# Narrower loads, half-block inversion in two groups and 512-token units in a recurrent-attention and feed-forward kernel

## The chip, the cores and the metric

The kernel runs on one core of one Trainium2 chip. The metric is the device time in microseconds (us) of one execution; lower is better. The engines are named as the profile names them: PE (TensorE matmul), PEld (TensorE weight load), DVE (VectorE), ACT (ScalarE), POOL (GpSimd) and SP (SyncE, which here only issues DMAs).

## The reference, cut to what matters

Two parts follow each other. The first is a recurrence over 768 tokens for each of 4 x 8 heads with a 40 x 40 state; the second multiplies its 3072 x 320 output through two up-projections, an elementwise product and a down-projection of width 1536 (weights in 64-bit floats).

```python
for t in range(S):                                    # S = 768, D = 40
    y[:, :, t] = np.einsum('bhd,bhde->bhe', rt, state)
    Sa = np.einsum('bhde,bhe->bhd', state, at)
    state_decay = state * wt[:, :, None, :] - np.einsum('bhd,bhe->bhde', Sa, bt)
    state = state_decay + np.einsum('bhd,bhe->bhde', vt, kt)
...
a = x @ w_a; b = x @ w_b; out = (a * b) @ w_out       # x: 3072 x 320, d_ff = 1536
```

## The kernel before, in words

**Attention in chunks.** The 768 tokens are cut into `NS` = 12 chunks of `C` = 64. Within a chunk the recurrence becomes matrix products and the inverse of a unit triangular 64 x 64 matrix for each head. Each chunk is handled in two parts c = 0, 1 (`NP`) of 16 heads, so there are 24 pairs (n, c), numbered q. In SBUF two heads share the 128 partitions: each half of 64 rows holds the 40 channels of a head and 24 rows of padding.

- `prep(n, c)` loads `W` (decays), `BK` (b and k) and `A` (a), runs two scans over the decays on DVE, scales the inputs, forms the score matrices on PE (`scores`), copies them to `AB` and `TK`, transposes `BK` on PE (`nat`, with the helper `transp`), and writes five results to a scratch area `un_d` in DRAM. `size` squares and sums two of them on ACT for a check of range.
- `lanes(g)` inverts the 32 x 32 diagonal blocks of two chunks at once (`GROUPS`: six groups of two): a transpose on DVE to `Nt`, then 31 steps of one multiplication and one subtraction on DVE over `Yt` (rows `Wt` are named Yt in the profile), then two transposes, `TC` and `T3` (named T in the profile). The code holds a second form, taken for the groups in `HALVED` (empty before): 15 steps over two 16 x 16 blocks at once, after which `join(n)` builds the 32 x 32 inverse on PE in three stages (`xt`, `t3`, `tc_`), with ACT copies between them.
- `merge(n)` builds the 64 x 64 inverse `T` from the 32 x 32 ones with two stages of small matmuls (`l2a`, `l2b`).
- `main(n, c)` loads `un_d` back (`UN`), v by token (`SV`, through `load_v`) and r, v by channel (`RV`), copies the state `ST` into the rest of `SV` on ACT (`s0`), and computes in turn `r_`, `u_`, the new state (`s_`, DVE), `g_`, `y_` and the outputs `X`, which go through DRAM (`x_d`) so that `pack(n)` can lay out the feed-forward input `xk` (its high and low parts).

**Feed-forward in units.** `unit` takes one tile f of 128 of the 1536 columns (`NF` = 12 tiles) and one chunk of 256 tokens: 16 matmuls into `ab` (2 x 8, 256 columns each), an ACT copy and a DVE product `g`, a rounded copy `gh` (ACT) and its remainder `gl` (POOL), and 6 matmuls of 320 columns into `po` (`second`). There are 144 units. The first `F1` = 5 tiles are done for each chunk while the attention runs; their sums go to DRAM (`po_d`) and come back as `acc` later. The other 7 tiles, in groups of `FG` = 2, run over all 12 chunks after the attention, and `xk` of the first 11 chunks is stored to `xk_d` and reloaded for this. The weights are decoded from 64-bit words by about six DVE and three ACT operations for each of three pieces of a tile (`decode`).

**Order.** Every operation is entered in a `Plan` with an engine, a cost and a priority v (lower first). The planner lays them out in advance, with its costs and four rotating PSUM banks `AT`; `AB2` (two banks) and `PO` (two banks) belong to the feed-forward. What results is a fixed order on each engine; all DMAs are issued by SP, in order, and an instruction that waits holds up those behind it. The constants `PV`, `PV1` (prep), `LV`, `LV0` (lanes; `LV0` for the first group), `MV` (join and merge), `UV` (units), `WV`, `WV1` (weights) set the priorities; `WG` names a key that the weight loads of the first tiles wait for.

Of the kernel before, what the change touches and what calls it, by code (L numbers as in the profile page):

```python
# [9 lines left out]
F32 = mybir.dt.float32  # L10
F32R = mybir.dt.float32r
# [40 lines left out]
PV, PV1, LV, MV, UV, WV, WV1 = -3.09, 0.6, -0.62, -0.34, 1.28, -1, 0.88  # L52
LV0 = -0.99
LIMIT = 2.0 ** 8
# [21 lines left out]
class Op:  # L76
    __slots__ = ("eng", "dur", "fn", "deps", "users", "v", "lat", "need", "free", "mode", "end", "left", "ready", "seq", "moved", "work", "port")


class Banks:  # L80


    def __init__(self, n):
        self.n, self.ids = n, None


# [23 lines left out]
class Plan:  # L110
# [41 lines left out]
    def run(self, slack=0.05, switch=0.13):  # L152
# [16 lines left out]
        while todo:  # L169
# [144 lines left out]
def wkv_moe(ctx, tc, wd, ai, bk, rvf, vn, pin, rv, wa, wb, wo, out):  # L314
# [32 lines left out]
    mul(PO[0][:, 320:512], fl, fr)  # L347

    def transp(ps, x):
        nc.tensor.matmul(ps, lhsT=x, rhs=ident, start=True, stop=True, is_transpose=True)  # L350

# [221 lines left out]
    XF = a1.tile([PK, 4, B * C], F32, name="XF")  # L573
    XK_ = ring(mp, 2, [PK, 6, B * C], "xk", F32R)


    nc0.vector.memset(D1, 0.0)
    for t in (*T_, *ST_, *RH_):
        nc0.gpsimd.memset(t, 0.0)
# [10 lines left out]
    def hd(x):  # L590
        return slice(C * x, C * x + D)

    def prep(n, c, v):
        q = n * NP + c
# [95 lines left out]
        pl.op("ACT", 1.6, size, [kPE, kQ], [kW], v=v + 0.5)  # L690

# [146 lines left out]
    def load_v(n, c, v):  # L838

        pl.dma(lambda: nc.sync.dma_start(out=SV_[c].rearrange("p g j i d -> p (g j i d)"), in_=vn[n, c]),  # L840
               begun(n), [("svv", c), ("svs", c)], 1.1, v=v)

    def main(n, c, v):
# [11 lines left out]
        load_v(n, c, v - 0.2)  # L855
        pl.dma(lambda: nc.sync.dma_start(
            out=RV.rearrange("p x m t -> p (x m t)"), in_=rvf[n, c]), begun(n), [kRV], 1.7, v=v - 0.2)
        if n:
# [98 lines left out]
        if n < NS - 1:  # L957
# [6 lines left out]
            pl.op("PE", 0.55, sd_, [kST], [("sd_", q), kSD], need=ps, work=1024, mode="t", lat=0.1, v=v + 0.3)  # L964
            pl.op("ACT", act(320), lambda ps=ps: nc.scalar.copy(
# [81 lines left out]
    for g in groups_of_chunks:  # L1047
# [7 lines left out]
        for x, n in enumerate(g):  # L1055
# [6 lines left out]
            pack(n, n + 0.3)  # L1062
            if n < NS - 1:
                pl.dma(lambda n=n: nc.sync.dma_start(out=xk_d[n], in_=XK_[n % 2].bitcast(F32)),
                       [("xk", n)], [("xkd", n), ("xkr", n % 2)], 2.4, v=n + 0.5)
                for f in range(F1):
                    unit(lambda n=n: XK_[n % 2], ("xk", n), slots[f], f, f == 0, f == F1 - 1, fin1(n), n + UV + f / F1)
# [8 lines left out]
               + [(k, x) for k in ("TC", "T3") for x in range(2)] + [("AB", x, c) for x in range(NAB) for c in range(NP)])  # L1076
    xk2 = {}
    ep = None
    NE = min(NS - 1, 4)

    def early():
# [3 lines left out]
        for i in range(FE):  # L1085
            slots[F1 + i] = weight_tiles(ep, F1 + i)
        for n in range(NE):
            xk2[n] = ep.tile([PK, 6, B * C], F32R, name=f"xk2_{n}")
    pl.op("-", 0.0, early, [], keys_pp + ["early"], lat=0.0, v=0)
# [11 lines left out]
    def late():  # L1101
        nonlocal xp
        actx.close()
        xp = lctx.enter_context(tc.tile_pool(name="xp", bufs=1, reuse_waits="tile"))
        for n in range(NE, NS - 1):
            xk2[n] = xp.tile([PK, 6, B * C], F32R, name=f"xk2_{n}")
        for n in range(NS):
            acc[n] = xp.tile([P, 2, DM], F32, name=f"acc{n}")

    def load_x(n, v):  # L1110
        pl.dma(lambda: nc.sync.dma_start(out=xk2[n].bitcast(F32), in_=xk_d[n]),
               [("xkd", n), "early" if n < NE else "late"], [("xk2", n)], 2.4, v=v)
# [6 lines left out]
    def run_tail():  # L1119
        pl.op("-", 0.0, late, [], keys_a + ["late"], lat=0.0, v=0)  # L1120
        for n in range(NS - 1):
            load_x(n, NS + 0.1 * n)

# [84 lines left out]
    for kk, fs in enumerate(groups):  # L1208
        last = kk == len(groups) - 1
        for n in range(NS):  # L1210
            if kk == 0 and n == ahead:
# [14 lines left out]
    def judge():  # L1226

        tot = const.tile([P, 1], F32, name="tot")
        nc.vector.tensor_reduce(out=tot, in_=sizes, axis=mybir.AxisListType.X, op=ALU.add)
        mul(AT[0][0:1, 0:1], tot, ones)  # L1230
        nc.vector.tensor_scalar(
            out=usual, in0=AT[0][0:1, 0:1], scalar1=LIMIT, scalar2=None, op0=ALU.is_lt)
    pl.op("PE", 0.5, judge, ["early", "late"], ["judge"], v=NS + 3, mode="j")

# [50 lines left out]
def layout(r, k, v, w, a, b, moe_w_a, moe_w_b, moe_w_out):  # L1285
# [35 lines left out]
    hv = heads(v).transpose(0, 1, 2, 6, 4, 3, 5, 7).reshape(ns, NP, 2, C, DM)  # L1321
    vn = np.zeros((ns, NP, 2, C, 2, DM), np.float32)
    for g in range(2):
        vn[:, :, 1 - g, :, g] = hv[:, :, g]
    vn = vn.reshape(ns, NP, P, 2 * DM)

# [51 lines left out]
```

## Time and profile before

| quantity | value |
|---|---|
| median of 3 runs | 842.21 us (841.82 to 847.74) |
| the profiled execution | 844.49 us; its span from first to last instruction 842.8 us |
| busy: PE, PEld, DVE, ACT, POOL | 690.6, 650.2, 570.4, 396.2, 167.4 us |
| granted TensorE clock, mean | 0.902 |
| DMA | 156.58 MB in 102018 packets, 186 GB/s |

Busy times overlap, so they do not add up to the span. A time in brackets behind an instruction is how long its engine stood idle before it, with what released it. The line number L70 is that of a helper through which every instruction is issued, so the rows are told apart by the tiles that they write and read.

### The profile page before, as it was taken

Reading aid. Unit: us, or ns where it says so; the run is one execution under the profiler, and the core shown is the slowest. Engines: PE = TensorE matmul, PEld = TensorE weight load, DVE = VectorE, ACT = ScalarE, POOL = GpSimd, SP = SyncE. Lnnn points to the kernel's source line nnn. Section 1 sums busy time; section 2 is a strip of 40 time slices with the busy share of each in tenths; the row PEclk is TensorE's granted clock in tenths of the full one; section 3 lists DMA queues with packets and bytes.
Section 4 is the critical chain, followed back from the end, with each engine's and each line's share of the span. In section 5 each row is a group of like instructions: output and inputs, shape, how many; then the busy total and the mean of one; then the engine's idle time right before and its main releaser. Section 6 shows DMA issues by size and latency. Waiting matters only on the chain.

```text
span 842.8 us, 29196 instructions
## 1 busy us (share of the span) xinstructions
PE 690.6 (82%) x12539; PEld 650.2 (77%) x12539; DVE 570.4 (68%) x1175; ACT 396.2 (47%) x1027; POOL 167.4 (20%) x217
## 2 busy tenths in 40 slices
PE   4332658657889968988899889989979999999996
PEld 3232547556789867877798889879969999999996
DVE  8689788898889858877897784366337665322343
ACT  4423757248454744475547455455425444222221
POOL 3000000100011200110011111145426554222221
PEclk9555877956999989999999999999989999999998
DMA  8892888957866778868886767876972220000023
GB/s 249 250 346 82 257 281 258 312 141 244 294 215 206 200 245 278 284 182 276 276 285 180 232 207 181 275 234 187 223 182 56 56 56 5 1 2 1 1 80 112
DMA packets 102018, 156.58 MB, mean 186 GB/s; under 512 B 30250, under 2 KB 70250, under 8 KB 98810
## 3 DMA queue, kind: packets, MB, share of 16 engines
q1 hardware_dynamic: 101882, 154.64, 60.4%
q8 instruction: 100, 1.64, 0.8%
q14 instruction: 36, 0.29, 0.1%
HBM read 101.97 MB, written 48.78 MB: 179 GB/s over the span
## 4 chain that ended last, share of the span: by engine, by line
PE 53%; DMA 22%; DVE 10%; ACT 6%; issue 5%; SPq 2%; POOL 1%; ACTq 0%; DVEq 0%; POOLq 0%
PE ab L70 25%; PE at L70 16%; PE po L70 12%; DMA SV<-in_vn_dram 6%; DMA XF<-x_d 3%; DMA x_d<-X 3%; DMA wraw<-in_wo_dram 2%; DVE Yt L70 2%; DVE Y L70 2%; DMA acc<-po_d 2%; SPq L70 2%; DMA wraw<-in_wa_dram 2%; DMA un_d<-A 2%; ACT SV L70 1%; DMA un_d<-bkn 1%
## 5 line engine op out<-in xcount | busy, mean ns | idle before, releaser
L70 PE MATMUL ab<-xk,wt 120*128 120x256 f32 x2304 | 311.3, 288 | 9.1 <-DVE g L70 8.3
L70 PEld LDWEIGHTS ab<-xk,wt 120*128 120x128 f32 x2304 | 294.5, 194 | 12.6 <-DVE g L70 8.7
L70 POOL TENSOR_TENSOR gl<-g,gh 128x256 fp32r<-128x256 f32 x144 | 113.9, 793 | 537.6 <-ACT gh L70 535.0
L70 DVE TENSOR_TENSOR g<-ab,g 128x256 f32<-128x256 f32 x144 | 60.8, 423 | 150.9 <-ACT g L70 150.5
L70 PE MATMUL po<-wo,gh 128*128 128x320 f32 x576 | 153.7, 317 | 0.7 <-DVE acc L70 0.7
L70 ACT COPY g<-ab 128x256 f32<-128x256 f32 x144 | 53.7, 373 | 154.8 <-PE ab L70 154.3
L70 PEld LDWEIGHTS po<-wo,gh 128*128 128x128 f32 x576 | 103.2, 190 | 2.7 <-ACT gh L70 1.0
L70 PE MATMUL po<-wo,gl 128*128 128x320 f32 x288 | 90.6, 314 | 0.8 <-POOL gl L70 0.6
L70 ACT CAST gh<-g 128x256 fp32r<-128x256 f32 x144 | 58.1, 405 | 54.6 <-DVE g L70 49.8
L70 PE MATMUL at<-SV,un 128*64 128x40 f32 (+1 forms) x1472 | 53.1, 235 | 32.2 <-ACT w_rs L70 9.0
L70 PEld LDWEIGHTS at<-SV,un 128*64 128x64 f32 (+1 forms) x1472 | 47.0, 145 | 39.2 <-issue 13.6
L70 DVE TENSOR_TENSOR Y<-Y,Yt 128x31 f32<-128x31 f32 (+15 forms) x186 | 65.4, 352 | 6.4
L70 DVE TENSOR_TENSOR Yt<-Y,N 128x31 f32<-128x31 f32 (+15 forms) x186 | 64.6, 347 | 4.6
L70 PEld LDWEIGHTS po<-wo,gl 128*128 128x128 f32 x288 | 55.1, 191 | 2.4 <-POOL gl L70 1.9
L70 PE MATMUL at<-A,BK 64*64 64x64 f32 x1536 | 36.3, 258 | 17.7 <-DVE A L70 16.2
L70 PE MATMUL at<-ident,BK 128*128 128x128 f32 x192 | 33.7, 324 | 19.2 <-DVE TK L70 7.0
L70 PEld LDWEIGHTS at<-A,BK 64*64 64x64 f32 x1536 | 32.6, 169 | 21.7 <-issue 13.8
L70 DVE TENSOR_TENSOR acc<-po,acc 128x320 f32<-128x320 f32 x96 | 42.6, 482 | 5.5 <-PE po L70 5.5
L70 ACT COPY SV<-ST 64x160 f32<-64x160 f32 x88 | 28.5, 323 | 37.6 <-DMA SV<-in_vn_dram 35.1
L70 PEld LDWEIGHTS at<-ident,BK 128*128 128x128 f32 x192 | 25.7, 165 | 22.8 <-DVE TK L70 7.9
L70 ACT COPY SV<-at 64x160 f32<-64x160 f32 x96 | 27.5, 287 | 25.3 <-PE at L70 24.0
L70 PE MATMUL at<-T,AB 32*32 32x32 f32 x768 | 17.0, 204 | 25.3 <-DVE T L70 23.1
(91 smaller groups left out, 1050.3 us busy)
## 6 DMA issues: line engine op xcount, KB each, us to landing
un<-un_d SPq DMA_DIRECT2D x24, 1092.0 KB
BK<-in_bk_dram SPq DMA_DIRECT2D x24, 512.0 KB
rv<-in_rvf_dram SPq DMA_DIRECT2D x24, 512.0 KB
xk_d<-xk SPq DMA_DIRECT2D x11, 720.0 KB
xk<-xk_d SPq DMA_DIRECT2D x11, 720.0 KB
un_d<-bkn SPq DMA_DIRECT2D x24, 320.0 KB
SV<-in_vn_dram SPq DMA_DIRECT2D x24, 320.0 KB
W<-in_wd_dram SPq DMA_DIRECT2D x24, 260.5 KB
```

Of the source, the lines that this page charges most:

```text
L70: r = fn(*args, **kwargs)
```

## The change

- **Loads.** For chunks after the first, `W`, `BK`, `A` and `RV` are loaded by a new helper `load` as two DMAs of 48 rows (`RL`) instead of one of 128. v by token loses its zero half in DRAM: `load_v` issues two DMAs of 64 rows by 1280 bytes instead of one of 128 by 2560, and no longer writes the part of `SV` that the state is copied to. `size` writes its by-product over `Q` instead of `W`.
- **Inversion.** `HALVED` names the groups 0 and 1 (chunks 0 to 3): 15 steps and `join` for them, 31 steps for the other four groups as before.
- **Units.** Behind the attention, `unit2` takes two chunks (512 tokens) for one tile: 16 matmuls of 512 columns, evictions of 512 columns, and 12 matmuls of 320 columns into four `po` banks, the eight with `gh` first and the four with `gl` last. It uses all eight PSUM banks, so all four `AT` banks are taken (`grab`) after the range check (`judge`), which moves ahead of it. The first two chunks with tiles 5 and 6 and the five units of the last chunk stay at 256 tokens, which leaves 40 `unit2`. Chunk 10 is no longer stored and reloaded; `xk` tiles lie in pairs.
- **Transpositions.** `transp` uses 104 rows and columns instead of 128.
- **Order.** New priorities, a planner cost for each PE instruction (`FETCH`, `NI`), and the first weight loads wait for the scores of q = 3 instead of q = 1.

```diff
+RL = 48
-WG = [("sc", 1)]
+WG = [('sc', 3)]
+P256 = 2
-HALVED = ()
+HALVED = (0, 1)
-PV, PV1, LV, MV, UV, WV, WV1 = -3.09, 0.6, -0.62, -0.34, 1.28, -1, 0.88
-LV0 = -0.99
+PV, PV1, LV, MV, UV, WV, WV1 = -3.13, 0.38, -0.8, -0.7, 1.13, -0.41, 0.72
+LV0 = -3
...
     def transp(ps, x):
-        nc.tensor.matmul(ps, lhsT=x, rhs=ident, start=True, stop=True, is_transpose=True)
+        nc.tensor.matmul(ps[:, 0:RU], lhsT=x[0:RU], rhs=ident[0:RU, 0:RU], start=True, stop=True, is_transpose=True)
...
+    def load(what, n, r, w, moved, v=None):
+        def go():
+            out, src = what()
+            if n == 0:
+                nc.sync.dma_start(out=out, in_=src)
+                return
+            for j in range(2):
+                sl = slice(C * j, C * j + RL)
+                nc.sync.dma_start(out=out[sl], in_=src[sl])
+        pl.dma(go, r, w, moved if n == 0 else moved * RL / C, 0.42 if n == 0 else 0.84, v=v)
...
     def load_v(n, c, v):
-        pl.dma(lambda: nc.sync.dma_start(out=SV_[c].rearrange("p g j i d -> p (g j i d)"), in_=vn[n, c]),
-               begun(n), [("svv", c), ("svs", c)], 1.1, v=v)
+        def go():
+            for g in range(2):
+                nc.sync.dma_start(
+                    out=SV_[c][half(1 - g), g].rearrange("p j i d -> p (j i d)"), in_=vn[n, c, g])
+        pl.dma(go, begun(n), [("svv", c)], 0.6, 0.84, v=v)
...
+    pl.op("PE", 0.5, judge, ["early", "late"], ["judge"], v=NS + 3, mode="j")
+    pl.op("-", 0.0, lambda: None, ["judge"], ["grab"], need=Banks(4), lat=0.0, v=0)
+    PO4 = PO + AT[2:4]
...
+    def unit2(pr, w, slot, first, last, lastg, v):
+        bk_ = [t.rearrange("p j t -> p (j t)") for t in AB2] if i == 0 else AT[0:2]
...
+                mul(o, wt[:, j, kw, :], xk2[pr][:, :, kxi, :], k == 0, k == 7)
...
+            for lo in range(2):
+                for b in range(4):
+                    po, sl = PO4[b][:, :DM], slice(b * P, (b + 1) * P)
+                    if lo:
+                        mul(po, mo2["gl"][i][:, sl], wot[:, 0, :], False, last)
+                    else:
+                        mul(po, mo2["gh"][i][:, sl], wot[:, 0, :], first, False)
+                        mul(po, mo2["gh"][i][:, sl], wot[:, 1, :], False, False)
...
+            if kk == 0 and n < P256:
+                for k, f in enumerate(fs):
+                    unit(xof(n), kx(n), W(slot_of(f)), slot_of(f), k == 0, k == len(fs) - 1, fin2(n, last), t)
+                    t += step
+            elif n % 2:
+                for k, f in enumerate(fs):
+                    unit2(n // 2, W(slot_of(f)), slot_of(f), k == 0, k == len(fs) - 1, last, t)
+                    t += step
```

More of the change, by code (lines that the diff above doesn't have):

```diff
@@ L76 @@
 class Op:
-    __slots__ = ("eng", "dur", "fn", "deps", "users", "v", "lat", "need", "free", "mode", "end", "left", "ready", "seq", "moved", "work", "port")
+    __slots__ = ("eng", "dur", "fn", "deps", "users", "v", "lat", "need", "free", "mode", "end", "left", "ready", "seq", "moved", "work", "port", "ni")
 class Banks:
@@ L84, in __init__ @@
         self.n, self.ids = n, None
+FETCH = 0.0016
+NI = {"half": 16, "second": 12, "scores": 128, "nat": 8, "r_": 64, "u_": 128, "s_": 64, "g_": 128, "y_": 128, "sd_": 8,
+      "l2a": 128, "l2b": 128, "xt": 258, "t3": 128, "tc_": 256}
 class Clock:
@@ L573, in wkv_moe @@
     XF = a1.tile([PK, 4, B * C], F32, name="XF")
-    XK_ = ring(mp, 2, [PK, 6, B * C], "xk", F32R)
+    XK2 = mp.tile([PK, 2, 6, B * C], F32R, name="xk")
+    XK_ = [XK2[:, i] for i in range(2)]
     nc0.vector.memset(D1, 0.0)
-    for t in (*T_, *ST_, *RH_):
+    for t in (*T_, *ST_, *RH_, *SV_):
         nc0.gpsimd.memset(t, 0.0)
@@ L689, in prep @@
             out=un[:, 16 * C + CW:], in_=BN.rearrange("p m j d -> p (m j d)")), [(*kBN, 0), (*kBN, 1)], [("un", q, 4)], 1.1, v=v + 0.3)
-        pl.op("ACT", 1.6, size, [kPE, kQ], [kW], v=v + 0.5)
+        pl.op("ACT", 1.4, size, [kPE], [kQ], v=v + 0.5)
     def lanes(g, v, halved):
@@ L855, in main @@
         load_v(n, c, v - 0.2)
-        pl.dma(lambda: nc.sync.dma_start(
-            out=RV.rearrange("p x m t -> p (x m t)"), in_=rvf[n, c]), begun(n), [kRV], 1.7, v=v - 0.2)
+        load(lambda: (RV.rearrange("p x m t -> p (x m t)"), rvf[n, c]), n, begun(n), [kRV], 1.7, v=v - 0.2)
         if n:
@@ L1086, in early @@
             slots[F1 + i] = weight_tiles(ep, F1 + i)
-        for n in range(NE):
-            xk2[n] = ep.tile([PK, 6, B * C], F32R, name=f"xk2_{n}")
+        for n in range(0, NE, 2):
+            xk2[n // 2] = ep.tile([PK, 2, 6, B * C], F32R, name=f"xk2_{n}")
     pl.op("-", 0.0, early, [], keys_pp + ["early"], lat=0.0, v=0)
@@ L1104, in late @@
         xp = lctx.enter_context(tc.tile_pool(name="xp", bufs=1, reuse_waits="tile"))
-        for n in range(NE, NS - 1):
-            xk2[n] = xp.tile([PK, 6, B * C], F32R, name=f"xk2_{n}")
+        for n in range(NE, NS - 2, 2):
+            xk2[n // 2] = xp.tile([PK, 2, 6, B * C], F32R, name=f"xk2_{n}")
+        xk2[NS // 2 - 1] = XK2
+        for x in ("g", "gh", "gl"):
+            mo2[x] = [xp.tile([P, 2 * 256], F32R if x in ("gh", "gl") else F32, name=f"{x}2{i}") for i in range(2)]
         for n in range(NS):
@@ L1121, in run_tail @@
         for n in range(NS - 1):
-            load_x(n, NS + 0.1 * n)
+            if n < NS - 2:
+                load_x(n, NS + 0.1 * n)
             def ld(n=n):
@@ L1197, in xof, with judge @@
     def xof(n):
-        return (lambda: XK_[n % 2]) if n == NS - 1 else (lambda: xk2[n])
+        return (lambda: XK_[n % 2]) if n >= NS - 2 else (lambda: xk2[n // 2][:, n % 2])
     def kx(n):
-        return ("xk", n) if n == NS - 1 else ("xk2", n)
+        return ("xk", n) if n >= NS - 2 else ("xk2", n)
+    def judge():
+        tot = const.tile([P, 1], F32, name="tot")
+        nc.vector.tensor_reduce(out=tot, in_=sizes, axis=mybir.AxisListType.X, op=ALU.add)
+        mul(AT[0][0:1, 0:1], tot, ones)
+        nc.vector.tensor_scalar(
+            out=usual, in0=AT[0][0:1, 0:1], scalar1=LIMIT, scalar2=None, op0=ALU.is_lt)
@@ new lines, in wkv_moe, with half, second @@
+    pl.op("PE", 0.5, judge, ["early", "late"], ["judge"], v=NS + 3, mode="j")
+    pl.op("-", 0.0, lambda: None, ["judge"], ["grab"], need=Banks(4), lat=0.0, v=0)
+    n2 = 0
+    PO4 = PO + AT[2:4]
+    def unit2(pr, w, slot, first, last, lastg, v):
+        nonlocal n2
+        i = n2 % 2
+        n2 += 1
+        kab = [("ab", 0), ("ab", 1)] if i == 0 else [("at", 0), ("at", 1)]
+        bk_ = [t.rearrange("p j t -> p (j t)") for t in AB2] if i == 0 else AT[0:2]
+        wt, wot = w
+        wk = [("wt", slot, 0), ("wt", slot, 1), ("wf", slot), ("wh", slot, 0), ("wh", slot, 1)]
+        def half(j):
+            o = bk_[j].rearrange("p (n t) -> p n t", n=2)
+            for k, (kw, kxi) in enumerate(KT):
+                mul(o, wt[:, j, kw, :], xk2[pr][:, :, kxi, :], k == 0, k == 7)
+        for j in range(2):
+            pl.op("PE", 1.81, lambda j=j: half(j), [kx(2 * pr), kx(2 * pr + 1), "grab", "late"] + wk, [kab[j]], v=v, work=7680, mode="r", lat=0.1)
+        pl.op("ACT", 0.62, lambda: nc.scalar.copy(out=mo2["g"][i], in_=bk_[0]), [kab[0]], [("g2", i)], v=v - 0.4)
+        pl.op("DVE", 0.7, lambda: nc.vector.tensor_mul(out=mo2["g"][i], in0=bk_[1], in1=mo2["g"][i]),
+              kab, [("g2", i)], v=v - 0.4)
+        pl.op("ACT", 0.63, lambda: nc.scalar.copy(out=mo2["gh"][i], in_=mo2["g"][i]), [("g2", i)], [("gh2", i)], v=v - 0.4)
+        pl.op("POOL", 1.38, lambda: nc.gpsimd.tensor_sub(out=mo2["gl"][i], in0=mo2["g"][i], in1=mo2["gh"][i].bitcast(F32)),
+              [("g2", i), ("gh2", i)], [("gl2", i)], v=v - 0.4, port=True)
+        def second():
+            for lo in range(2):
[6 more added lines that the diff above has]
+                        mul(po, mo2["gh"][i][:, sl], wot[:, 1, :], False, False)
+        pl.op("PE", 1.76, second, [("gh2", i), ("gl2", i), ("wt", slot, 2), ("wh", slot, 2)], [("po", b) for b in range(4)],
+              v=v - 0.2, work=7680, mode="r", lat=0.1)
+        if last:
+            for b in range(4):
+                n, hf = 2 * pr + b // 2, b % 2
+                pl.op("DVE", 0.5, lambda b=b, n=n, hf=hf: nc.vector.tensor_add(
+                    out=acc[n][:, hf, :], in0=PO4[b][:, 0:DM], in1=acc[n][:, hf, :]), [("po", b)], [("acc", n, hf)], v=v - 0.4)
+                if lastg and hf:
+                    pl.dma(lambda n=n: nc.sync.dma_start(out=out[n].rearrange("f p d -> p f d"), in_=acc[n]),
+                           [("acc", n, 0), ("acc", n, 1)], [("out", n)], 1.1, v=v - 0.4)
@@ L1224, in wkv_moe @@
             planned += 1
[L1226 to L1233, printed above, removed]
     pl.run()
@@ L1321, in layout @@
     hv = heads(v).transpose(0, 1, 2, 6, 4, 3, 5, 7).reshape(ns, NP, 2, C, DM)
[L1322 to L1325, printed above, removed]
+    vn = np.ascontiguousarray(hv)
     order = [h for t in KHEADS for h in t]
```

29 lines of the change are left out of this document (15 added, 14 removed).

## The prediction

> **What bounds the kernel now.** I read the page first, then the stages by window (busy time of each engine, granted clock, DMA share), then the chain of work inside the second stage.
>
> ```profile
> PE 690.6 (82%) x12539; PEld 650.2 (77%) x12539; DVE 570.4 (68%) x1175; ACT 396.2 (47%) x1027; POOL 167.4 (20%) x217
> ...
> 0.00:76.00 76.00, 23.81 (x425) 20.41 (x425) 61.93 (x124) 25.64 (x63) 7.25 (x21) 0.63 0.78 248
> 76.00:138.00 62.00, 41.48 (x1204) 36.99 (x1208) 52.08 (x92) 41.58 (x106) 1.11 (x2) 0.72 0.80 246
> 138.00:172.00 34.00, 21.79 (x470) 19.80 (x460) 28.09 (x73) 11.83 (x34) 2.66 (x3) 0.86 0.80 263
> 172.00:238.00 66.00, 47.14 (x1262) 41.99 (x1262) 57.47 (x106) 39.93 (x105) 2.86 (x4) 0.79 0.79 235
> 640.00:843.00 203.00, 195.38 (x1538) 194.66 (x1537) 90.97 (x205) 68.92 (x170) 74.25 (x91) 0.99 0.12 36
> ```
>
> 82% of PE is a mean over unlike stages. Up to 238 us (four chunks of attention) DVE is busy 81 to 87% of each window, PE 31 to 71%, and the DMA engines 78 to 80%. Behind 640 us PE is busy 96% and DVE 45%: only PE work shortens that stage. What the first stages wait for shows in the chain of work, its shares over the span first and then its DMA pieces from 83 us on:
>
> ```profile
> PE 53%; DMA 22%; DVE 10%; ACT 6%; issue 5%; SPq 2%; POOL 1%; ACTq 0%; DVEq 0%; POOLq 0%
> ...
> 83.07 2.41 DMA un_d<-A
> 85.57 3.81 DMA un_d<-bkn
> 97.78 5.15 DMA SV<-in_vn_dram
> 116.20 9.61 DMA SV<-in_vn_dram
> ```
>
> The chain goes through DMAs, not through DVE: SP issues in order and waits for a buffer to be stored before it loads the next. So DVE is nearly full and yet not alone the bound, which decides how much of a DVE saving arrives.
>
> **The first group's inversion.**
>
> ```profile
> 30.33 0.69 DVE L70 TENSOR_TENSOR A<-A,pe 128x512 f32<-128x512 f32 x1 [1.42 <-DMA A<-in_ai_dram]
> 36.57 2.13 DVE L70 STREAM_TRANSPOSE N<-AB 128x1024 f32<-128x1024 f32 x1
> 49.81 0.18 DVE L70 TENSOR_TENSOR Yt<-Y,N 128x31 f32<-128x31 f32 x1
> 75.83 1.92 DVE L70 STREAM_TRANSPOSE T<-Y 128x1024 f32<-128x1024 f32 x1
> L70 DVE TENSOR_TENSOR Y<-Y,Yt 128x31 f32<-128x31 f32 (+15 forms) x186 | 65.4, 352 | 6.4
> L70 DVE TENSOR_TENSOR Yt<-Y,N 128x31 f32<-128x31 f32 (+15 forms) x186 | 64.6, 347 | 4.6
> L70 DVE TENSOR_TENSOR Y<-Y,Yt 128x135 f32<-128x135 f32 x12 | 3.6, 300 | 0.4
> L70 DVE TENSOR_TENSOR Y<-Y,Yt 128x31 f32<-128x31 f32 x12 | 2.4, 203 | 0.4
> 77.89 1.92 PE L70 MATMUL at<-T,AB 32*32 32x32 f32 x64 [15.09 <-DVE T L70]
> L70 ACT ACTIVATE T<-at 32x512 f32<-32x512 f32 x24 | 14.1, 588 | 5.2 <-PE at L70 4.9
> ```
>
> Until 77.75 us (75.83 + 1.92) no chunk can be merged; PE waits 15.09 us for it.
>
> - Steps now: (65.4 + 64.6)/6 groups = 21.7 us of DVE a group. A halved step works on 2(s+1)(15-s) elements, 1360 in all over 15 steps. The rows of 31 and 135 elements (203 and 300 ns) give 174 ns + 0.93 ns an element, so 15 x 174 + 0.93 x 1360 = 3.9 us for each of the two operations, 7.75 us. Two products over 128 x 512 come on top, 0.69 each by the A row. Saved: 21.7 - 7.75 - 1.4 = **12.5 us of DVE a group**.
> - `join` adds, per chunk, 321 matmul records (a small f32 product shows as two: 64 records are the 32 products of `l2a`). At 1.92/64 = 30 ns that is 9.6 us of PE at the start's low clock, and four ACT evictions of 512 columns (0.59 each, 2.3 us): about **12 us in line** for the chunk that waits.
> - `LV0` = -3 and `WG` put the first lanes ahead of chunk 2's prep and of the first weights, which now fill 38.7 to 49.8. I put the transpose N at 34 us (36.57 less about half of the 6.2 us since the A product): 34 + 2.1 + 1.4 + 7.75 + 3.9 (two transposes) = 49, + 12 = 61 to 62, against 77.75: 16 us. The decoding of one tile moves behind (about 10 us of DVE), while a prep of about 6 us moves forward into the join's shadow: 4 us come back at 84% busy. **Term 1: -13**; with the N where it was, -10; with no displaced work, -18.
> - Group 1 saves the same 12.5 us of DVE at 83 to 87% busy, and its first join stands 12 us in line where PE has a third to spare. **Term 2: -9** (0 if SP's chain sets the pace, -15 if DVE's does, 12.5/0.84). What would be late next is the DMA chain above.
> - The other three joins lie on PE in stages where it idles 30%: **+2** (0 to +9).
>
> **The loads.**
>
> ```profile
> BK<-in_bk_dram SPq DMA_DIRECT2D x24, 512.0 KB
> rv<-in_rvf_dram SPq DMA_DIRECT2D x24, 512.0 KB
> SV<-in_vn_dram SPq DMA_DIRECT2D x24, 320.0 KB
> W<-in_wd_dram SPq DMA_DIRECT2D x24, 260.5 KB
> ACT SV L70 <- DMA SV<-in_vn_dram: 35.1, 13, 8.4
> L70 SPq DMA_DIRECT2D W<-in_wd_dram x24: 339/516/1400, 0.8 to 400.6; - x24
> SPq L70 <- PE at L70: 68.5, 39, 5.7
> ```
>
> A pair (n, c) drops a quarter of BK, rv, W and A (A has 128 x 512 words, 256 KB) and half of SV: 385 + 160 = 545 KB of the 6.5 MB that a twenty-fourth of all traffic is, a twelfth. The state's copy on ACT waits 35.1 us for the v load, 13 times, because the load writes the whole of SV. After the change the halves are apart: the copy can run ahead, and PE alone waits for v. The wait itself does not vanish, as `r_` needs v; what leaves the path is the pair of copies behind it and a twelfth of the queue ahead. I take 0.75 us of each of the 13 waits. **Term 3: -10**; bounds 0 (PE is late anyway) and -35 (the whole wait).
>
> SP issues 88 + 24 = 112 DMAs more, at the W row's median 0.52 us: 58 us of SP's time; it is at present idle for long waits such as the 68.5 us for PE, so most of it is hidden. **+3** (0 to +58).
>
> [...]
>
> **The units behind the attention.**
>
> ```profile
> 722.07 2.08 PE L70 MATMUL ab<-xk,wt 120*128 120x256 f32 x16
> 723.99 0.31 PE L70 MATMUL po<-wo,gh 128*128 128x320 f32 x1
> 724.87 1.36 PE L70 MATMUL ab<-xk,wt 120*128 120x256 f32 x10
> L70 POOL TENSOR_TENSOR gl<-g,gh 128x256 fp32r<-128x256 f32 x144 | 113.9, 793 | 537.6 <-ACT gh L70 535.0
> L70 DVE TENSOR_TENSOR g<-ab,g 128x256 f32<-128x256 f32 x144 | 60.8, 423 | 150.9 <-ACT g L70 150.5
> L70 ACT CAST gh<-g 128x256 fp32r<-128x256 f32 x144 | 58.1, 405 | 54.6 <-DVE g L70 49.8 <-PE po L70 3.7
> 619.69 0.33 DVE L70 TENSOR_SCALAR w_ex<-wraw 128x320 int32<-128x320 int32 x1 [8.25 <-DMA wraw<-in_wo_dram]
> 621.52 2.08 PE L70 MATMUL ab<-xk,wt 120*128 120x256 f32 x8 [6.24 <-DVE g L70]
> ```
>
> A unit takes 724.87 - 722.07 = 2.80 us: 16 matmuls in 1.92 us (120 ns each) and 6 in 0.88 (147). The 64 columns between the two shapes cost 26.7 ns, 0.417 a column, so 13.3 ns stay per matmul. 512 columns then take 226.7 ns, and a `unit2` 16 x 226.7 + 12 x 146.7 = 5.39 us against 5.60 for two units. 40 of them: **term 4: -8.5**. [...]
>
> The evictions must fit beneath the next unit's first 16 matmuls (3.63 us): doubled rows give at most 0.85 (DVE) + 0.81 (ACT) + 1.59 (POOL) = 3.25 us, and `gl` is needed only after eight more matmuls. PE stays the bound.
>
> At 615 us PE stood still 6.24 us, because DVE's queue was held 8.25 us by a weight word behind the reloads. One chunk less is reloaded: **-2** (0 to -9). Against this, all four `AT` banks must be free first; nine 256-token units (25 us) cover that.
>
> Transpositions: 24/128 of the work of
>
> ```profile
> L70 PE MATMUL at<-ident,BK 128*128 128x128 f32 x192 | 33.7, 324 | 19.2 <-DVE TK L70 7.0 <-DVE BK L70 4.3 <-ACT AB L70 3.3
> ```
>
> is 6 us, a quarter of it where PE bounds: **-1.5**.
>
> **Sum.** -13 - 9 + 2 - 10 + 3 - 8.5 - 2 - 1.5 = -39. The profiled execution took 844.5 us (span 842.8), which gives 805.5; the runs' median lies 2.3 lower, so **803 us**.
>
> **Rivals.**
>
> 1. **SP's chain sets the pace of the attention.** For it: the chain quoted from 83 us on runs through DMAs and SP; against it: DVE at 81 to 87%. Then term 1 halves to -7, term 2 goes, term 3 shrinks to -3, the rest stays at -10: 844.5 - 20 - 2.3 = 822, up to 838 if the joins also cost.
> 2. **DVE sets it entirely.** Then terms 1 and 2 become -18 and -15, term 3 reaches -20, the stall goes (-9): 803 - 28 = 775. Against it: the same chain.
> [...]
> 4. **Slower: SP becomes the bound.** The 112 added issues (58 us) lie on the path where SP has no wait left; it decides once SP is busy or blocked throughout the attention. Then 803 + 50 = 853. Against it: the 68.5 us that SP waits for PE alone.
>
> **Numbers.** Forecast 0.57 (787 to 820 by its own terms), rival 1: 0.22, rival 2: 0.11, rival 3: 0.04, rival 4: 0.06. The range 780 to 832 takes in the forecast, most of rivals 1 and 3 and the nearer half of 2. About 1% (8.4 us) is what a measurement can tell from no change: faster 0.87 (all but rival 4 and the top of rival 1), within it 0.07, slower 0.06.
>
> **What would show it.** The pack of the fourth chunk, the first that lies behind both halved groups, begins now at
>
> ```profile
> 272.25 1.57 ACT L70 CAST xk<-XF 120x512 fp32r<-120x512 f32 x3 [1.38 <-DMA XF<-x_d]
> ```
>
> Right: the first T transpose ending near 50 and the first `l2a` near 62 us; 22 to 25 us less DVE time in Y and Yt; ACT's wait for the v load gone and PE's small; a steady pitch of 5.39 us behind the attention; the DMA total down by 22 x 385 KB + 24 x 160 KB + 1.4 MB for chunk 10, some 14 MB. Wrong, if that pack comes less than 10 us earlier, if PE waits for banks or `gl` between units, or if SP is without waits up to 500 us.

## The result, and the profile after

The changed kernel takes 854.38 us in the median (844.99 to 868.96, 20 runs) against 842.39 for the kernel before (835.0 to 851.18, 20 runs): a ratio of 1.0132, interval 1.0097 to 1.0168, **slower by 1.3%**. The forecast was 803. A ratio here and below leaves out every execution more than 1.5% above the fastest of its kernel, so that it can differ from the ratio of two medians.

The page of the changed kernel first: busy time of the engines, DMA queues (packets, MB, share of 16 engines), and the shares of the chain of work.

```profile
PE 710.4 (83%) x13183; PEld 642.6 (75%) x13183; DVE 540.7 (63%) x1075; ACT 389.7 (46%) x967; POOL 163.2 (19%) x185
DMA packets 100729, 142.58 MB, mean 167 GB/s; under 512 B 32012, under 2 KB 75084, under 8 KB 97516
q8 instruction: 105, 1.72, 0.9%
PE 51%; DVE 16%; DMA 15%; issue 7%; ACT 6%; SPq 4%; POOL 1%; DVEq 0%; ACTq 0%; POOLq 0%
```

Both kernels fall into two stretches, cut at the pack of the last chunk. This is the ACT row that begins a `pack`, for the first and the last chunk before, then for the first, the fourth and the last after.

```profile
138.07 1.56 ACT L70 CAST xk<-XF 120x512 fp32r<-120x512 f32 x3
581.00 1.57 ACT L70 CAST xk<-XF 120x512 fp32r<-120x512 f32 x3
```

```profile
138.74 1.58 ACT L72 CAST xk<-XF 120x512 fp32r<-120x512 f32 x3 [1.12 <-DMA XF<-x_d]
281.26 1.57 ACT L72 CAST xk<-XF 120x512 fp32r<-120x512 f32 x3 [1.64 <-DMA XF<-x_d]
600.99 1.58 ACT L72 CAST xk<-XF 120x512 fp32r<-120x512 f32 x3 [1.64 <-DMA XF<-x_d]
```

The attention ends 20.0 us later (600.99 against 581.00). What follows it takes 842.8 - 581.0 = 261.8 us before and 853.1 - 601.0 = 252.1 after, 9.7 less. 20.0 - 9.7 = 10.3 us is the whole difference of the two spans. So the loss lies in the attention alone. Busy time to the last pack, by window (columns as in the prediction), before and then after:

```profile
0.00:581.00 581.00, 442.46 (x10608) 403.25 (x10609) 451.71 (x909) 303.82 (x801) 68.28 (x97) 0.87 0.77 237
```

```profile
0.00:601.00 601.00, 465.64 (x11863) 426.42 (x11864) 427.22 (x851) 310.10 (x816) 71.19 (x103) 0.88 0.73 207
```

DVE does 24.5 us less work, as worked out, and PE 23.2 more. The stretch is longer although its fullest engine has less to do: 78% busy before became PE 77% and DVE 71%. Nothing became a new bound by its load. Waits grew instead. First before, then after (total us, times, longest):

```profile
DVE BK L70 <- DMA BK<-in_bk_dram: 8.9, 6, 4.5
DVE Q L70 <- DMA W<-in_wd_dram: 5.0, 4, 2.0
PE at L70 <- issue: 23.4, 21, 2.9
```

```profile
PE at L72 <- issue: 43.1, 24, 4.6
DVE BK L72 <- DMA BK<-in_bk_dram: 21.2, 7, 6.1
ACT Q L72 <- DVE BK L72: 18.7, 8, 6.6
DVE Q L72 <- DMA W<-in_wd_dram: 16.4, 7, 5.2
PE at L72 <- DMA SV<-in_vn_dram: 11.8, 1, 11.8
```

ACT's 35.1 us for v are gone. DVE now waits 37.6 us for BK and W (13.9 before), and PE's time without a named releaser rose by 19.7 us.

The early inversion came much as the prediction had it; what follows it did not. From the timeline of DVE, the transpose N, the first and the last halved step, and the transpose T. Then from PE's, the three stages of the first `join` (`xt` at 55.70, `t3` at 67.07, `tc_` at 76.75), two rows of score products (`at<-A,BK`) that stand between them, and the first products of `merge` (`l2a`, 64 records as before, at 85.87):

```profile
38.91 2.12 DVE L72 STREAM_TRANSPOSE N<-AB 128x1024 f32<-128x1024 f32 x1
42.34 0.18 DVE L72 TENSOR_TENSOR Yt<-Y,N 128x30 f32<-128x30 f32 x1
50.76 0.21 DVE L72 TENSOR_TENSOR Y<-Y,Yt 128x30 f32<-128x30 f32 x1
52.87 1.94 DVE L72 STREAM_TRANSPOSE T<-Y 128x1024 f32<-128x1024 f32 x1
```

```profile
55.70 1.93 PE L72 MATMUL at<-T,AB 32*32 32x32 f32 x128
62.43 1.43 PE L72 MATMUL at<-A,BK 64*64 64x64 f32 x41 [3.95 <-issue]
67.07 1.20 PE L72 MATMUL at<-W,TC 32*32 32x32 f32 x64
74.72 2.10 PE L72 MATMUL at<-A,BK 64*64 64x64 f32 x64 [4.94 <-DVE BK L72]
76.75 1.93 PE L72 MATMUL at<-TC,W 32*32 32x32 f32 x128
85.87 1.92 PE L72 MATMUL at<-T,AB 32*32 32x32 f32 x64 [4.30 <-ACT TC L72]
```

T ends at 54.8 against 77.75, 23 us earlier. But the first `l2a` begins at 85.87 against 77.89, 8.0 us later than before: the join takes 31.1 us in line. The first pack comes at 138.74 against 138.07. The chain of work shows what stands behind T:

```profile
58.48 3.95 issue
62.43 4.78 PE at L72 x113
...
69.49 3.81 DMA BK<-in_bk_dram
...
77.04 4.94 DMA BK<-in_bk_dram
...
91.03 4.87 DMA wraw<-in_wb_dram
```

The score products of the next preps now stand in PE's queue between the stages of the first join and ahead of its merge. The rows at 62.43 and 74.72 are two of them. The first waits 3.95 us for nothing that the profile names; the second waits for a BK load that lands at 73.30. The copy of `tc_` on ACT then stands behind the squares of a prep whose BK lands only at 81.98. The queues run in order (the products of `tc_` end at 78.68, and their copy starts at 85.23, behind 3.83 us in which ACT stood idle for that BK), so join, merge and `main(0)` wait with them.

### The profile page after: what moved, and what is told of

It reads as the page before. It is cut to its first block, busy times and chain, and to the rows that moved or that the text cites. A ratio compares the mean times of both kernels' runs of the same rounds, so it can differ in the third digit from the quotient of the medians.

```text
span 853.1 us, 30406 instructions
## 1 busy us (share of the span) xinstructions
PE 710.4 (83%) x13183; PEld 642.6 (75%) x13183; DVE 540.7 (63%) x1075; ACT 389.7 (46%) x967; POOL 163.2 (19%) x185
## 2 busy tenths in 40 slices
DMA packets 100729, 142.58 MB, mean 167 GB/s; under 512 B 32012, under 2 KB 75084, under 8 KB 97516
## 3 DMA queue, kind: packets, MB, share of 16 engines
q1 hardware_dynamic: 100588, 140.57, 58.0%
q8 instruction: 105, 1.72, 0.9%
## 4 chain that ended last, share of the span: by engine, by line
PE 51%; DVE 16%; DMA 15%; issue 7%; ACT 6%; SPq 4%; POOL 1%; DVEq 0%; ACTq 0%; POOLq 0%
PE at L72 25%; PE ab L72 18%; PE po L72 8%; SPq L72 4%; DMA XF<-x_d 3%; DVE Yt L72 3%; DVE Y L72 3%; DMA BK<-in_bk_dram 2%; DVE G L72 2%; DMA W<-in_wd_dram 2%; DMA x_d<-X 1%; DVE BK L72 1%; DVE Q L72 1%; DMA SV<-in_vn_dram 1%; ACT xk L72 1%
## 5 line engine op out<-in xcount | busy, mean ns | idle before, releaser
L72 PE MATMUL ab<-xk,wt 120*128 120x256 f32 (+1 forms) x1344 | 232.6, 327 | 0.5 <-DVE g L72 0.3
L72 POOL TENSOR_TENSOR gl<-g,gh 128x256 fp32r<-128x256 f32 (+1 forms) x104 | 103.4, 995 | 577.3 <-ACT gh L72 566.0
L72 PEld LDWEIGHTS ab<-xk,wt 120*128 120x128 f32 x1344 | 201.0, 205 | 14.4 <-DVE g L72 0.5
L72 PE MATMUL po<-wo,gh 128*128 128x320 f32 x416 | 102.5, 324 | 7.8 <-ACT gh L72 7.5
L72 ACT CAST gh<-g 128x256 fp32r<-128x256 f32 (+1 forms) x104 | 50.6, 487 | 106.6 <-DVE g L72 106.1
L72 DVE TENSOR_TENSOR g<-ab,g 128x256 f32<-128x256 f32 (+1 forms) x84 | 40.6, 484 | 81.1 <-ACT g L72 60.9
L72 PE MATMUL at<-xk,wt 120*128 120x512 f32 x320 | 76.8, 392 | 0.0
L72 PEld LDWEIGHTS at<-xk,wt 120*128 120x128 f32 x320 | 59.6, 188 | 12.6
L72 DVE TENSOR_TENSOR Y<-Y,Yt 128x31 f32<-128x31 f32 (+20 forms) x154 | 51.9, 337 | 5.3
L72 DVE TENSOR_TENSOR Yt<-Y,N 128x31 f32<-128x31 f32 (+20 forms) x154 | 52.9, 344 | 3.6
L72 PE MATMUL at<-ident,BK 104*128 104x104 f32 x192 | 29.6, 302 | 17.5 <-DVE TK L72 9.5
L72 PEld LDWEIGHTS po<-wo,gl 128*128 128x128 f32 x208 | 38.6, 194 | 4.2 <-POOL gl L72 4.0
```

Source lines behind the costliest of these rows:

```text
L72: r = fn(*args, **kwargs)
```

## The experiments

All were timed in five rounds against the kernel before (841 to 843 us in these batches). *units* is the kernel before with `unit2` alone. "Order held" means that the planner's figures (costs, priorities) were left as they were, so that each engine gets its work in the same order; otherwise the planner lays the order out anew.

| kernel | median us | ratio to before | interval |
|---|---|---|---|
| a_whole | 853.34 | 1.0136 | 1.0065 to 1.0207 |
| a_steps31 | 871.21 | 1.0342 | 1.0275 to 1.0408 |
| a_oldorder | 860.12 | 1.0196 | 1.0131 to 1.026 |
| b_units | 838.34 | 0.9969 | 0.9931 to 1.0007 |
| u_half | 851.95 | 1.0015 | 0.9974 to 1.0055 |
| u_size | 875.03 | 1.0394 | 1.0349 to 1.0439 |
| u_vn | 851.08 | 1.0101 | 1.0052 to 1.015 |
| h_all | 837.91 | 0.9861 | 0.9805 to 0.9918 |
| h_narrow | 837.68 | 1.0004 | 0.9966 to 1.0041 |
| c_uv | 849.69 | 1.0107 | 1.0067 to 1.0148 |
| c_pv1 | 847.23 | 1.006 | 1.0021 to 1.0099 |
| c_mv | 842.07 | 1.0061 | 1.0007 to 1.0115 |
| a_pv1 | 877.8 | 1.0455 | 1.0389 to 1.052 |
| a_pvm | 865.72 | 1.0333 | 1.0262 to 1.0404 |
| a_junk | 856.52 | 1.0192 | 1.0119 to 1.0265 |
| a_nojoin | 850.01 | 1.0101 | 1.0037 to 1.0165 |
| u_fewsteps | 826.44 | 0.9807 | 0.9744 to 0.987 |

### Whole parts of the changed kernel undone

**a_whole**: the channel loads in one DMA of 128 rows again; the planner's figures as they were.

```diff
-            if n == 0:
-                nc.sync.dma_start(out=out, in_=src)
-                return
-            for j in range(2):
-                sl = slice(C * j, C * j + RL)
-                nc.sync.dma_start(out=out[sl], in_=src[sl])
+            nc.sync.dma_start(out=out, in_=src)
```

> The changed kernel with its planned order untouched, but each channel load issued as one DMA of 128 rows in place of two of 48 (88 issues fewer, 8.5 MB more). SP theory (the doubled issues hold SP, busy 65% in place of 50%, and so delay buffers): 835 to 842 us, 12 to 20 below the changed kernel, and SP busy back near 55%. Join theory (the joins' small matmuls load PE and its instruction fetch): within 5 us of the changed kernel. Order theory (the new priorities spend the early start on preps): within 5 us of it.

The 88 issues are gone, 8.67 MB more are moved, and the time stayed (1.0136 against 1.0132, within about 1%). Rival 4, SP as the bound, falls, and the narrow loads, bytes and issues taken together, are not what costs.

**a_steps31**: no group is halved (`HALVED = ()`), all else as in the changed kernel.

> The changed kernel with no group halved: 31 steps everywhere and no join. Join theory: 840 to 847 us, PE's waits for nothing that the profile shows down from 43 to some 23 us, in spite of 25 us more of DVE. SP theory and order theory: 855 to 870, since DVE gets its 25 us back and SP stays as it is.

With these priorities the halving is a gain of 2.1% (17.7 us), although the planner lays the order out anew here too. The loss lies elsewhere, and is larger than 1.3%.

**a_oldorder**: priorities, `WG`, `LV0` and `FETCH` as before the change.

```diff
-WG = [('sc', 3)]
+WG = [("sc", 1)]
-PV, PV1, LV, MV, UV, WV, WV1 = -3.13, 0.38, -0.8, -0.7, 1.13, -0.41, 0.72
-LV0 = -3
+PV, PV1, LV, MV, UV, WV, WV1 = -3.09, 0.6, -0.62, -0.34, 1.28, -1, 0.88
+LV0 = -0.99
-FETCH = 0.0016
+FETCH = 0
```

> The changed kernel with the priorities, the key of the weight loads and the planner's PE costs of before (PV, PV1, LV, LV0, MV, UV, WV, WV1, WG as before, FETCH 0). Order theory: 835 to 845 us, the pack of chunk 0 before 130 us. SP theory and join theory: 850 to 860.

1.0196 against 1.0132, with overlapping intervals: the old figures do not bring the old order back, since the changed costs of loads, joins and transpositions lay it out anew as well. The first pack, expected before 130 us, comes at 155.41.

### One part at a time, order laid out anew

**b_units**: `unit2`, its tiles and the chunk that stays in SBUF; nothing else.

> The kernel before with the 512-token units alone (and chunk 10 kept in SBUF): loads of 128 rows, 31 steps, transpositions of 128, the old order. All theories: the stage behind the attention shortens by 8 to 12 us at a pitch near 5.4 us for two units, the attention ends within 5 us of before, and the whole takes 830 to 836. If it takes 840 or more, the units cost something at the changeover that the sum left out.

The median fell by 4 us, the ratio by 0.3%, at the limit of what shows and less than the 8 to 12 us expected. Behind its last pack the profiled execution spends 253.5 us against 261.8, so the stage shortens where it was forecast. This execution took 828.44 us, 10 us less than the median, and comparisons with its trace below have that margin.

```profile
573.20:826.70 253.50, 243.00 (x1293) 213.63 (x1291) 116.84 (x227) 78.90 (x148) 89.88 (x80) 0.99 0.24 71
```

**u_half**: units and `HALVED = (0, 1)`.

> The kernel before with the 512-token units and, of the rest, only the halved inversion of groups 0 and 1 (old order, loads of 128 rows). If halving is a gain by itself (it was worth 18 us within the changed kernel): 815 to 825 us. If the joins' PE time and instruction fetch eat it: 836 to 845.

+0.5% on units by the ratios (1.6% by the medians): in this order the 25 us of DVE that go buy nothing. The trace shows one reason at the first chunk: T ends at 64.0 us against 77.5 in units, but the first `l2a` begins at 87.04 against 77.67. The join takes 23.0 us in line, more than the 13.5 us by which T comes earlier. The joins also bring PE waits with them; the row of its waits, against 21.4 us in units:

```profile
PE at L72 <- issue: 41.9, 26, 4.3
```

**u_size**: units, and the squares written over `Q` with the dependences and the cost of the changed kernel.

```diff
-                    out=W[:, 0:CW], in_=t, func=AF.Square, scale=2.0 ** -30,
+                    out=Q[:, 0:CW], in_=t, func=AF.Square, scale=2.0 ** -30,
-        pl.op("ACT", 1.6, size, [kPE, kQ], [kW], v=v + 0.5)
+        pl.op("ACT", 1.4, size, [kPE], [kQ], v=v + 0.5)
```

> The 512-token units and, of the rest, only the range check's squares written over Q instead of W. In the changed kernel ACT stands 18.7 us in front of this operation until DVE has multiplied BK. Theory of the by-product (ACT, in order, is held by it, and the next scan on DVE waits for ACT): 848 to 860 us. Theory of the loads: within 5 us of 838.

+4.2% on units, for an edit that removes work. Either ACT now holds `Q` too long, or the order did it; a_junk below bears on this.

**u_vn**: units, and v in two DMAs of 64 rows.

```diff
-        pl.dma(lambda: nc.sync.dma_start(out=SV_[c].rearrange("p g j i d -> p (g j i d)"), in_=vn[n, c]),
-               begun(n), [("svv", c), ("svs", c)], 1.1, v=v)
+        def go():
+            for g in range(2):
+                nc.sync.dma_start(
+                    out=SV_[c][half(1 - g), g].rearrange("p j i d -> p (j i d)"), in_=vn[n, c, g])
+        pl.dma(go, begun(n), [("svv", c)], 0.6, 0.84, v=v)
```

> The 512-token units and, of the rest, only v by token in two DMAs of 64 rows that leave the state's half of SV alone. My term 3 gave this nearly the whole gain of the loads: 828 to 833 us. If the wait only passes to PE: 836 to 842. Above 846 it is a loss by itself.

+1.3% on units, with half the bytes and no wait of ACT's for v. The part that was to gain 10 us lost 11 in this order.

**u_loads**: units, and channel loads of 48 rows, with the squares still over `W`.

```diff
-            nc.sync.dma_start(out=out, in_=src)
+            if n == 0:
+                nc.sync.dma_start(out=out, in_=src)
+                return
+            for j in range(2):
+                sl = slice(C * j, C * j + RL)
+                nc.sync.dma_start(out=out[sl], in_=src[sl])
```

> The 512-token units and, of the rest, only the loads as two DMAs of 48 rows, planned as such. Theory of the loads (SP's time, and a plan that counts on quicker landings): 848 to 860 us. Theory of the by-product: 833 to 840.

8078 us: the squares leave their values in the rows of `W` that are no longer reloaded, the check of range trips, and the slow path by token runs behind the attention, as DVE's 12920 instructions on its page show. The run says nothing on the loads, only why the squares had to move.

```profile
PE 5061.1 (63%) x19675; PEld 2486.2 (31%) x19675; DVE 6477.0 (80%) x12920; ACT 1179.8 (15%) x2591; POOL 158.7 (2%) x186
```

### The order alone

Five kernels change a single priority by 0.02 and no work.

```diff
 c_uv, on units:   UV   1.28 -> 1.26
 c_pv1, on units:  PV1  0.60 -> 0.58
 c_mv, on units:   MV  -0.34 -> -0.32
 a_pv1, on after:  PV1  0.38 -> 0.40
 a_pvm, on after:  PV1  0.38 -> 0.36
```

> The 512-token units, with the priority UV of the units nudged from 1.28 to 1.26: the same work in another order. Order theory: 845 to 865 us, the last pack 10 to 30 us later, though nothing was added. Parts theory: within 4 us of 838.

> As c_uv, with PV1 (prep of a group's second chunk) nudged from 0.60 to 0.58; the order differs from about the middle of the attention on. Order theory: 843 to 860 us. Parts theory: within 4 us of 838.

> As c_uv, with MV (merge) nudged from -0.34 to -0.32; the order differs from about the middle of the attention on. Order theory: 843 to 860 us. Parts theory: within 4 us of 838.

> The changed kernel with PV1 nudged from 0.38 to 0.40: the same work, another order from the start. Order theory: anywhere between 840 and 875 us, off the changed kernel by 5 us or more. By-product theory: within 5 us of 854.

> The changed kernel with PV1 nudged from 0.38 to 0.36: the same work, another order from about a quarter on. Order theory: anywhere between 840 and 875 us. By-product theory: within 5 us of 854.

All five are slower: by 0.9 to 1.4% of units (8 to 12 us; an interval of each is 0.4 to 0.5 wide on either side), by 2.0 and 3.2% of the changed kernel (17 and 27 us). c_mv is the least sure, with 0.5% by the medians. An order can be worth more than any part of this change. Where a nudge loses shows in the packs of the eighth and the last chunk, first in units, then in c_uv:

```profile
434.26 1.57 ACT L72 CAST xk<-XF 120x512 fp32r<-120x512 f32 x3 [0.75 <-DMA XF<-x_d]
573.22 1.56 ACT L72 CAST xk<-XF 120x512 fp32r<-120x512 f32 x3
```

```profile
444.38 1.58 ACT L72 CAST xk<-XF 120x512 fp32r<-120x512 f32 x3 [0.45 <-DMA XF<-x_d]
586.52 1.57 ACT L72 CAST xk<-XF 120x512 fp32r<-120x512 f32 x3
```

The two executions differ by 21.8 us, 13.3 of them ahead of the last pack. The medians differ by 11 us only, as the profiled execution of units lies 10 us below its median.

### The parts with the order held

**h_all**: units, narrow v, narrow BK, A and r/v (not W, which still takes the squares), transpositions of 104.

```diff
-        nc.tensor.matmul(ps, lhsT=x, rhs=ident, ...)
+        nc.tensor.matmul(ps[:, 0:RU], lhsT=x[0:RU], rhs=ident[0:RU, 0:RU], ...)
-            nc.sync.dma_start(out=out, in_=src)
+            if n == 0 or w[0][0] == "W":
+                nc.sync.dma_start(out=out, in_=src)
+                return
+            for j in range(2):
+                sl = slice(C * j, C * j + RL)
+                nc.sync.dma_start(out=out[sl], in_=src[sl])
 ...
```

> The 512-token units with the order of instructions on every engine kept as it is there (planner's costs and keys untouched), but v in two DMAs of 64 rows, BK, A and RV in two of 48 (W whole, as the squares still go over it), and transpositions of 104. Order theory (each part costs mainly because it makes the planner lay out another order, and the order of before is a good one): 830 to 838 us, no part a loss. Parts theory (narrow v and narrow loads lose by themselves, as u_vn and u_loads seemed to show): 850 to 870.

0.9861: by the ratio 1.1% below units and 1.4% below the kernel before, the lowest of a kernel that does all the work. By the medians (837.91 against 838.34 for units and 837.68 for h_narrow below) the three are alike, so a gain of these parts is not shown; that they lose nothing in the held order is. The wait of ACT for v is gone and PE's share of it is 10.5 us; PE's waits without a named releaser are shorter than in units (21.4):

```profile
PE at L72 <- issue: 15.6, 13, 3.8
...
PE at L72 <- DMA SV<-in_vn_dram: 10.5, 2, 5.5
```

**h_narrow**: h_all with W narrow as well and the squares in a tile of their own (to make room, an unused constant goes).

```diff
-            if n == 0 or w[0][0] == "W":
+            if n == 0:
-                    out=W[:, 0:CW], in_=t, func=AF.Square, scale=2.0 ** -30,
+                    out=JK, in_=t, func=AF.Square, scale=2.0 ** -30,
```

> h_all with W narrow too (two DMAs of 48 rows), the squares in a scratch tile, the order still that of the kernel before: all of the change's loads, units and transpositions, without halving and without a new order. Order theory: 825 to 838 us, below both kernels. If narrow loads or the added issues cost by themselves: 845 or more.

1.0004, like units (0.9969) within the intervals, and by the ratio, not by the medians, 1.4% behind h_all. It does the work of a_steps31 (but for where the squares go) in the old order, so the two price the order. The stretch to the last pack, h_narrow and then a_steps31:

```profile
0.00:579.00 579.00, 445.32 (x10605) 408.07 (x10606) 449.46 (x908) 302.32 (x800) 69.81 (x99) 0.90 0.75 215
```

```profile
0.00:617.60 617.60, 450.44 (x10580) 411.80 (x10581) 451.95 (x911) 300.24 (x796) 67.35 (x97) 0.81 0.71 202
```

PE, DVE and ACT are busy for the same time within 5.1 us, and the second takes 38.6 us longer. By the timed ratios it is 1.0342 - 1.0004 = 3.4%, 28.5 us. The lower granted clock of the second (0.81 against 0.90) is not the reason: a_steps31 took 870.86 us in an execution with a mean clock of 0.916, and 871.56 in this one with 0.867.

**u_fewsteps**: units, with 13 of the 31 steps in each of the first two groups; 18 are left out, which takes as much of DVE as halving does, with no join.

```diff
+                    if g[0] < 4 and s % 5 not in (0, 2):
+                        return
```

> The 512-token units with the order kept, and 13 of the 31 inversion steps issued in groups 0 and 1 (the other 18 are left out, so the inverse is not complete): DVE loses some 25 us as with halving, and no join is added. If DVE sets the pace of the first stages, as terms 1 and 2 of the sum have it: 813 to 820 us, 18 to 25 below 838. If the chain through SP, DMA and PE sets it: 830 to 838.

1.6% below units, 13.7 us for some 24 us of DVE. The saving is real and a little over half arrives. Without a join the first `l2a` begins at 63.81, 13.9 us ahead of units. The packs of the first, the fourth and the last chunk show the lead, 15.1 us over units in the first (136.03 there), 13.9 in the fourth (268.06) and 4.3 in the last (573.22). So the second group adds nothing to the lead in these two executions. How much is given back later is not shown: the two profiled executions take the same time (spans 827.1 and 826.7), as that of units lies 10 us below its median.

```profile
120.98 1.58 ACT L72 CAST xk<-XF 120x512 fp32r<-120x512 f32 x3 [0.33 <-DMA XF<-x_d]
254.19 1.58 ACT L72 CAST xk<-XF 120x512 fp32r<-120x512 f32 x3 [1.03 <-DMA XF<-x_d]
568.94 1.57 ACT L72 CAST xk<-XF 120x512 fp32r<-120x512 f32 x3
```

**a_nojoin**: the changed kernel with the three product loops of `join` (`xt`, `t3`, `tc_`) cut to the first of 16 passes; the others are left out.

```diff
-            for cm in range(NP * M):
+            for cm in range(1):
```

> The changed kernel with the order kept, and each stage of the join cut to the first of its 16 products per block (the rest is left out, so the 32 x 32 inverse is not built): PE loses some 24 us of small matmuls and their instruction fetches, ACT and DVE nothing. If the joins cost +2 as in the sum: 850 to 856 us. If PE's order in the attention is full enough that they cost their whole time and the fetch waits: 815 to 835.

1.0101 against 1.0132: 2.6 us, within the intervals. Only products are left out; the three stages, their copies and what stands between them stay, and the first `l2a` begins at 84.39 instead of 85.87. So the run prices the joins' PE work, not their place in line. PE's waits without a named releaser fell by half, and still little came of it:

```profile
PE at L72 <- issue: 20.5, 17, 4.0
```

**a_junk**: the changed kernel with the squares in a tile of their own, order held.

```diff
-                    out=Q[:, 0:CW], in_=t, func=AF.Square, scale=2.0 ** -30,
+                    out=JK, in_=t, func=AF.Square, scale=2.0 ** -30,
```

> The changed kernel in its own order, with the range check's squares written to a scratch tile of their own instead of over Q (the tile is bf16, and an unused 192-column constant makes room). Nobody reads the squares themselves; their sums are unchanged. By-product theory (ACT, held 18.7 us before this operation, holds DVE and PE): 835 to 845 us. Order theory: 850 to 856, the wait moves elsewhere.

No gain (1.0192). The theory that the squares hold `Q` falls for the changed kernel; for u_size the order is then the likelier cause, but that was not tried by itself.

## Why the prediction was wrong, step by step

**The step that failed** is the one that read the new priorities and early lanes only as a gain (term 1) and left the rest of the order as good as it was. It put the first join at 12 us in line, where it took 31.1, and no term stood for a new order, where the runs show +28.5 us:

| from | to | ratio | us |
|---|---|---|---|
| before | h_narrow: units, all narrow loads and transpositions, old order | 1 to 1.0004 | 0 |
| h_narrow | a_steps31: the new order | to 1.0342 | +28.5 |
| a_steps31 | after: two groups halved, the order laid out anew again | to 1.0132 | -17.7 |

Each step carries about 0.7% (6 us) of uncertainty, the first 0.4%. The forecast had -19 us for the first step (units, loads, SP, stall, transpositions), nothing for the second and -20 for the third. That the third came out near its number is luck: with the old priorities the same halving gave +0.5% on units (u_half), and in both the first merge begins later than without halving (85.87 against 67.35 in a_steps31, 87.04 against 77.67 in units).

That the order is what costs is shown for the kernels that differ in it alone (the nudges) and, with the squares' place as the one remainder, for a_steps31. Which of its re-placements lose the time is not: the next preps between the stages of the first join are seen in the traces and were not undone alone. A halved kernel in the old order was not reached, since the halving changes the planner's costs (u_half).

- **Term 1 (-13).** Half of the mechanism held: the lane steps run from 42.34 to 50.97, 8.6 us where 7.75 was worked out, and T ends at 54.8 (forecast "near 50"). The other half failed: `l2a`, forecast near 62, begins at 85.87, later than the 77.89 of before. The 12 us in line were the join's own PE work and evictions added up. Its products take only some 6 us of PE, and leaving most of them out moved `l2a` by 1.5 us (a_nojoin). The time goes to the preps that stand between its stages and to the BK loads that these wait for. "What is late next" was named as the DMA chain; two of its pieces, 3.81 and 4.94 us for BK, stand there.
- **Term 2 (-9), with term 1 -22.** The saved DVE time is as computed, from the groups of the changed kernel: 52.9 + 51.9 = 104.8 us where the rows of before sum to 130.0.

```profile
L72 DVE TENSOR_TENSOR Y<-Y,Yt 128x31 f32<-128x31 f32 (+20 forms) x154 | 51.9, 337 | 5.3
L72 DVE TENSOR_TENSOR Yt<-Y,N 128x31 f32<-128x31 f32 (+20 forms) x154 | 52.9, 344 | 3.6
L72 PE MATMUL at<-ident,BK 104*128 104x104 f32 x192 | 29.6, 302 | 17.5 <-DVE TK L72 9.5 <-ACT AB L72 4.9 <-DVE BK L72 1.7
```

  The worth of both was mis-sized: 13.7 us with the order held and no join (u_fewsteps), not 22.
- **Joins (+2).** They add 23.2 us of PE, and this work is hidden as assumed: leaving it out gave 2.6. Their wait in line was not: 31.1 us for the first (23.0 in u_half).
- **Loads (-10) and SP (+3).** The DMA total fell by 156.58 - 142.58 = 14.0 MB and ACT's wait for v went, as forecast. No gain of them is shown: with the order held h_all lies 9 us below units by the ratio and level by the medians, and h_narrow, with W as well, is level with units. SP's issues, taken together with the smaller loads, cost nothing that shows (a_whole).
- **Transpositions (-1.5).** 33.7 to 29.6 us of PE, 4.1 where 6 were taken; too small to time.
- **Units (-8.5) and the stall (-2).** The mechanism is right, and the stage behind the last pack is 9.7 us shorter. Timed alone the units gave less, 2.6 us by the ratio and 4 by the medians (b_units). The chain behind the attention shows a pair of units, 800.55 - 789.73 = 10.82 us, 5.41 each (forecast 5.39):

```profile
789.73 1.84 PE ab L72 x8
791.57 0.59 PE po L72 x4
...
795.17 3.63 PE at L72 x16
...
800.55 1.84 PE ab L72 x8
```

  512 columns take 3.63/16 = 227 ns, as worked out from the shapes of before. 16 such matmuls take 3.63 us, where the 32 of 256 columns in two units of before take 2 x 1.92 = 3.84 us.
- **Rivals.** 1 (SP's chain) saw that half of the DVE saving would not arrive, but gave no loss. 3, a loss by the narrow loads themselves, is shown by no run: whole loads in their place changed nothing (a_whole, 1.0136 against 1.0132). 4 had the right sign and, with 853, nearly the number, for a wrong reason. Of the signs of being right, the DVE time, ACT's wait for v, the pitch behind the attention and the DMA total came; the first `l2a` near 62 did not. The marker that was to prove the forecast wrong did: the fourth chunk's pack comes at 281.26, 9.0 us later than before instead of 10 earlier.

## What to carry to other kernels

Where a planner writes a fixed order, every cost and priority that an edit touches lays the whole order out anew, and that can be worth more than the edit: nudges without any work moved this kernel by 1 to 3%. Give a new order a term of its own, of either sign, sized by a few such nudges, and test each part with the order held (the planner's figures untouched) before it is laid out anew. Do not price a chain of stages by adding up their work: in an in-order queue, what the planner puts between them counts as well (31.1 us here, where the forecast had added up 12). Read the first result behind an early gain, not the step itself.

## What the runs showed of the hardware

- **Narrower loads moved fewer bytes in the same DMA time.** The packets of queue q1 in a_whole and in the changed kernel, share of the span last:

```profile
q1 hardware_dynamic: 101996, 149.24, 58.5%
```

```profile
q1 hardware_dynamic: 100588, 140.57, 58.0%
```

  0.585 x 845.3 = 494.5 us and 0.580 x 853.1 = 494.8 us of 16 engines, for 149.24 and 140.57 MB. At a_whole's rate 8.67 MB are 28.7 us, and none of it was saved. If the other transfers took the same time in both, loads of 48 rows, with three quarters of the bytes, ran at about three quarters of the rate of 128 (an estimate). This fits with no gain of the loads being shown where the order was held.
- **Rows of small products stop PE with no releaser.** "PE at <- issue" is 12.2 us in h_narrow, 15.6 in h_all and 21.4 in units, 43.1 (after) and 41.9 (u_half) with joins, and 20.5 with most of the joins' products left out. Most of the long ones end some 2.4 us after a packet of 16 KB (1.72 MB / 105) on the instruction queue q8 starts, in the packet records (2.28 to 2.58 us in six of the eight over 2 us in the changed kernel): one starts at 60.0 us, the gap quoted above ends at 62.43. So they look like waits for instructions; that is seen, not tested. They are also not what made the kernel slower: with half of them gone it gained 2.6 us (a_nojoin).
